# Forgetting attention and channel mix: x of the first two chunks written straight into SBUF, the first chunk mixed pair by pair

## Chip, cores, metric

One core of a Trainium2 chip. The metric is the device time of one execution in microseconds (us); lower is better. TensorE does the matrix products, VectorE (DVE), ScalarE (ACT) and GpSimd (POOL) the rest; SyncE (SP) issues nearly all DMAs. SBUF is the memory on the core, PSUM the banks that TensorE writes.

## What is computed

A causal attention with a forget bias, for 8 batches, 8 heads, 576 tokens and 64 columns a head; its output, laid out as 576 tokens of 512 columns, goes through a channel mix:

```python
s_pos = np.maximum(s, 0.0)
cum = np.cumsum(s_pos, axis=-1)
bias = -(cum[:, :, :, None] - cum[:, :, None, :])
scores = np.where(causal, -1000000000.0, scale * q @ k.T + np.minimum(bias, 0.0))
attn = softmax(scores)                       # over the keys
x = attn @ v                                 # then laid out as [batch, token, 512]
x_prev = x shifted by one token (zero first)
xk = mu_k * x + (1.0 - mu_k) * x_prev
xr = mu_r * x + (1.0 - mu_r) * x_prev
k = np.maximum(xk @ w_k, 0.0)                # 512 -> 1024
out = sigmoid(xr @ w_r) * (k * k @ w_v)      # 1024 -> 512
```

## The kernel before

**Attention.** It runs in visits; a visit is one batch and one pair of heads (`hp`, four pairs a batch). Batch 0 is visited in two halves: first the query tiles A (tokens 0 to 319) of all four pairs, then Z (tokens 320 to 575) of all four; the other batches are visited once a pair. A visit computes scores (`scores`, L815: products on TensorE at L828 or L839, then VectorE at L856, exponentials on ScalarE at L874, normalising on GpSimd at L893), turns the weights and multiplies by the values. For the first twelve visits the turning is done by TensorE (L982, L997) and the value products by L956; from visit 12 on by VectorE (L920) into the tile `turned` (`turned_d`, 128 x 3840 words), DMAs and L1133. `blanks` (L511) clears parts of `turned_d` once; in the kernel before it does so at the start.

**x.** `weighted` (L972) ends in a ScalarE copy (L1095) of the value products from the PSUM bank `po` into the SBUF tile `xT`: columns are tokens, the 128 partitions are the channels of the pair. `finish` (L1453) writes `xT` to `x_d` in DRAM by DMA (L1461).

**Channel mix.** The 4608 tokens are cut into 18 chunks of 256 (`CT`). A chunk can start when the attention of its tokens is there for all four pairs, for chunk 0 after the four A visits, for chunk 1 after the four Z visits. `channel_mix` (L1165) loads x of all pairs by DMA from `x_d` (L1355), mixes it (`mix`, L1233): for each block `c` of 128 channels (which is one pair of heads) ScalarE multiplies by mu into a PSUM bank (L1193), VectorE adds the shifted part (L1204); then `splits` takes two blocks at once, a ScalarE copy rounds them to the high part `xh` (L1223) and VectorE subtracts for the low part `xl` (L1227). `mix(0)` feeds the hidden layer (L1256, 96 products a chunk), `mix(1)` the gate (L1298). The hidden layer is squared (L1268 to L1286) into `kh` and `kl`, which have one buffer, and multiplied by w_v (L1328). The weights w_k, w_r and w_v arrive as float64 words and are converted once by ScalarE, VectorE and GpSimd (`load_weight`, L626: L661 to L695); those of w_v use the tiles `x` and `r` and the bank `xp` on the way.

**Order.** Nothing is emitted in program order: each step is a task with an engine, a length, what it reads and writes and a due time, and `Plan.run` (L322) lists the tasks forty times, forward and backward, by its own model of lengths and gaps, and emits the best order found. Each engine then runs its own queue in that order. While TensorE would have nothing to do, the planner puts in dummy products on the identity matrix (`plan.idle`, L445, into bank `xp`), until the task `plan.busy_from`, which is the first mix of chunk 0 (L1201). `late` (L1496) orders the loads of w_v behind the x load of chunk 0 in the plan.

Of the kernel before, what the change touches and what calls it, by code (L numbers as in the profile page):

```python
# [337 lines left out]
def forgetting_attention_then_channel_mix(  # L338
# [15 lines left out]
    nc = tc.nc  # L354
# [148 lines left out]
    turned_d = fixed(const.tile([P, 4, NS, 32], F32, name="turned"))  # L503
    across = fixed(ph_both[:, 0 : 4 * NS * 32].rearrange("p (i s x) -> p i s x", i=4, s=NS))
    across.last = phs

    def slots(h, kb, t):

# [20 lines left out]
                [], [(t, ("h", kb))], 64, 36,  # L529
            )  # L530

    first_load = []
    late, LATE = [], ("v",)
    mu = fixed(const.tile([P, 2, NC], F32, name="mu"))
    mu1 = fixed(const.tile([P, 2, NC], F32, name="mu1"))
# [433 lines left out]
        )  # L969
        plan.columns[i] = 4 * n  # L970

    def weighted(pts, V, xT, tiles, blocks):  # L972


        def transposed(pt, ph):
# [186 lines left out]

    x_d = [fixed(dram.tile([P, NP, S + 1], F32, name=f"x_d{b}")) for b in range(B)]

    def channel_mix(ch, start, span):  # L1165
        t0 = ch * CT
        segs = []
        t = t0
# [6 lines left out]
        last = ch >= NCHUNK - 3  # L1175

        def at(x):
            plan.due = start + span * x

        def product_bank():  # L1180
            if not last:
# [3 lines left out]

        def mixed(which, c, y, xm):
            for i, (_, _, n, o) in enumerate(segs):

                def to(n=n, o=o):
                    return xm.get()[:, y * CT + o : y * CT + o + n]  # L1190

                first = act(
                    lambda n=n, o=o, i=i, to=to: nc.scalar.activation(  # L1193
                        to(),
                        x.get()[:, c, o + i + 1 : o + i + 1 + n],
                        AF.Copy,
                        scale=mu.ap[:, which, c : c + 1],
                    ),
                    [(x, i), (mu, which)], [(xm, (y, o)), (xm, "a")], n, 160, ports="S>P",
                )  # L1200
                if plan.busy_from is None:  # L1201
                    plan.busy_from = first
                dve(
                    lambda n=n, o=o, i=i, to=to: nc.vector.scalar_tensor_tensor(  # L1204
                        out=to(),
                        in0=x.get()[:, c, o + i : o + i + n],
                        scalar=mu1.ap[:, which, c : c + 1],
                        in1=to(),
                        op0=ALU.mult,
                        op1=ALU.add,  # L1210
                    ),
                    [(x, i), mu1], [(xm, (y, o)), (xm, "d")], n, ports="SP>P",
                )

        def splits(c, xm, hi, lo):
            parts = [(xm, (y, o)) for y in range(2) for _, _, _, o in segs]
            cc = slice(c, c + 2)

            def src():
                return xm.get().rearrange("p (c x) -> p c x", c=2)  # L1220

            act(
                lambda: nc.scalar.copy(hi.get()[:, cc], src()),  # L1223
                parts, [(hi, c), (hi, c + 1)], 2 * CT, ports="P>S",
            )
            dve(
                lambda: nc.vector.tensor_tensor(  # L1227
                    out=lo.get()[:, cc], in0=src(), in1=f32(hi.get()[:, cc]), op=ALU.subtract
                ),
                parts + [(hi, c), (hi, c + 1)], [(lo, c), (lo, c + 1)], 2 * CT, ports="PS>S",  # L1230
            )
# [129 lines left out]
        if ch == 0:  # L1361
            first_load.append(i_x)
        at(-MLEAD)
        mix(0)
        for fp in range(NF // 2):
            at(0.1 * fp)
            hidden(fp)
            if fp == 0:
                at(0.2)
                mix(1)  # L1370
        for tt in range(CT // P):
            at(0.4 + 0.1 * tt)
            gate(tt)
# [64 lines left out]
    prefix_sums()  # L1438
    plan.due = 25000.0
    constant_rows()  # L1440
    plan.due = 50000.0
    blanks()
    plan.due = 1000.0
    load_mu()
    for o in range(DF // 512):
# [7 lines left out]
    def finish(pts, V, xT, n, due):  # L1453
        b, hp, tiles = visits[n]
        plan.due = due
        weighted(pts, V, xT, tiles, n >= BLOCKS)
        q0, q1 = QS[tiles[0]], QS[tiles[-1]] + QN[tiles[-1]]

        c = slice(1 + q0 if q0 else 0, 1 + q1)
        dma(  # L1460
            lambda: nc.sync.dma_start(x_d[b].ap[:, hp, c], xT.get()[:, c]),  # L1461
            [(xT, -1)] + [(xT, x) for x, _ in sums_of(tiles)],
            [(x_d[b], (hp, y)) for y in range(2) if tiles is ALL or y == (q0 > 0)],
            1300 * (q1 - q0) / S,
        )
        if hp == NP - 1:
            there[b] = q1

    for n, (b, hp, tiles) in enumerate(visits):
        due = dues[n]  # L1470
        step = STEPS[tiles]
        plan.due = due - LEAD * step
        if 0 < n < len(visits) - 1:
            load(n + 1)
        plan.due = due
        xT = sbuf([P, S + 1], "xT", 1)
        pool(lambda xT=xT: nc.gpsimd.memset(xT.get()[:, 0:1], 0.0), [], [(xT, -1)], 2, 36)
        for j in range(2):
            plan.due = due + j * step
            pt = scores(b, 2 * hp + j, tiles, n >= BLOCKS, *QKs[n])  # L1480
            if j == 0:
                other = pt
            else:
                finish((other, pt), Vs[n], xT, n, due + (j + WDUE) * step)
            if j == 0 and n + 1 < len(visits):
                plan.due = due + SPLIT * step
                prepare(n + 1)
        while done_chunks < NCHUNK:
            end = (done_chunks + 1) * CT - 1
# [4 lines left out]
            channel_mix(done_chunks, chunk_due, CHUNK)  # L1494
# [47 lines left out]
```

## Time and profile before

| what | value |
|---|---|
| runs | 794.86 us median of 3 (793.86 to 796.66) |
| profiled execution | 793.36 us, of which the span 791.5 us |
| TensorE busy | 771.6 us, 97% of the span |
| weight loads of TensorE | 638.7 us, 81% |
| VectorE, ScalarE, GpSimd busy | 563.8, 472.1, 345.1 us |
| mean granted TensorE clock | 0.994 of full |
| DMA | 152.12 MB, mean 192 GB/s |

The span runs from the first to the last instruction of the profiled execution. A busy time is the sum of the instructions' durations; products that follow one another overlap in it. The granted clock has two levels, full (2.4 GHz, shown as 1.00) and half (1.2 GHz, shown as 0.50); a figure between is a mean over a stretch. Lines are those of the kernel before.

### The profile page before, as it was taken

How to read it: one execution, taken by the hardware profiler on the slowest of the kernel's cores; microseconds unless marked ns; L12 is line 12 of the kernel's file. 1: busy time of each engine (PE TensorE's matmuls, PEld its weight loads, DVE VectorE, ACT ScalarE, POOL GpSimd, SP SyncE). 2: the span in 40 equal slices, each digit the busy share in tenths (PEclk: the TensorE clock that was granted, in tenths of full speed). 3: DMA queues.
4: the chain of work that ended last, by engine and by line, in shares of the span. 5: the costliest groups of instructions: out<-in, count | busy, mean ns of one | idle time of the engine just before them, and what ended most of it. 6: DMA issues, size and time to landing. Idle time of an engine off the chain costs nothing.

```text
span 791.5 us, 16205 instructions
## 1 busy us (share of the span) xinstructions
PE 771.6 (97%) x5216; PEld 638.7 (81%) x5216; DVE 563.8 (71%) x1868; ACT 472.1 (60%) x1305; POOL 345.1 (44%) x620
## 2 busy tenths in 40 slices
PE   7999989999999999999999999999999999999998
PEld 5667867978887878788878888887888788788997
DVE  7987976668866877677777677668877787355521
ACT  5778988766744665465564666556645666345411
POOL 7996887543544444423344434343444421100000
PEclk9998999999999999999999999999999999999999
DMA  7887875688999888888888988899888776421000
GB/s 226 261 251 217 246 215 149 179 194 219 227 233 243 230 209 226 210 223 212 224 203 210 233 218 220 212 246 217 238 228 213 185 196 172 115 76 41 14 27 27
DMA packets 65701, 152.12 MB, mean 192 GB/s; under 512 B 13662, under 2 KB 27236, under 8 KB 65616
## 3 DMA queue, kind: packets, MB, share of 16 engines
q1 hardware_dynamic: 65456, 150.92, 73.4%
q8 instruction: 41, 0.67, 0.4%
q14 instruction: 44, 0.36, 0.1%
q10 hardware_dynamic: 160, 0.16, 0.1%
HBM read 51.34 MB, written 19.48 MB: 89 GB/s over the span
## 4 chain that ended last, share of the span: by engine, by line
PE 56%; SPq 12%; DVE 11%; DMA 6%; POOL 6%; ACT 5%; issue 4%; DVEq 0%; ACTq 0%; POOLq 0%
PE m L1256 16%; PE m L1328 12%; SPq L1104 11%; PE s L839 6%; PE po L1133 5%; PE m L1298 5%; DVE turned L920 3%; DMA ph<-turned 2%; POOL W L893 2%; DVE W L856 2%; PE po L956 2%; DVE xp L1204 2%; PE s L1328 2%; DMA x<-x_d 2%; ACT xp L1193 2%
## 5 line engine op out<-in xcount | busy, mean ns | idle before, releaser
L874 ACT ACTIVATE W<-W,nm 128x448 f32<-128x448 f32 (+4 forms) x320 | 178.6, 559 | 75.4 <-DVE nm L856 71.6
L1256 PE MATMUL m<-xh,w_k 128*128 128x256 f32 x1024 | 198.8, 283 | 0.5 <-DVE g L1338 0.5
L893 POOL TENSOR_SCALAR W<-W,rinv 128x192 f32<-128x192 f32 (+4 forms) x320 | 164.5, 529 | 26.8 <-DVE rinv L942 25.2
L1328 PE MATMUL m<-w_v,kh 128*128 128x512 f32 (+1 forms) x512 | 171.4, 394 | 0.0
L1256 PEld LDWEIGHTS m<-xh,w_k 128*128 128x128 f32 x1024 | 163.0, 188 | 2.9 <-DVE g L1338 0.9
L856 DVE CUSTOM_DVE_ANT_0 W<-s,causal 128x448 f32<-128x448 f32 (+5 forms) x320 | 130.4, 419 | 45.9 <-PE s L839 40.1
L1256 PE MATMUL m<-xl,w_k 128*128 128x256 f32 x512 | 144.1, 282 | 0.0
L920 DVE STREAM_TRANSPOSE turned<-W 128x64 f32<-128x64 f32 (+5 forms) x432 | 121.8, 327 | 28.8 <-DMA ph<-turned 11.7
L1193 ACT ACTIVATE xp<-x,mu 128x256 f32<-128x256 f32 (+3 forms) x172 | 72.4, 421 | 59.8 <-DMA x<-x_d 26.3
L1328 PEld LDWEIGHTS m<-w_v,kh 128*128 128x128 f32 x512 | 94.9, 189 | 15.4
L937 POOL TENSOR_SCALAR rinv<-sums 128x5 f32<-128x5 f32 (+2 forms) x72 | 17.2, 238 | 199.6 <-ACT W L874 193.2
L839 PE MATMUL s<-KH,G 128*64 128x64 f32 x336 | 98.1, 303 | 5.3 <-DVE nm L856 4.2
L1328 PE MATMUL m<-w_v,kl 128*128 128x512 f32 (+1 forms) x256 | 101.3, 396 | 0.0
L839 PE MATMUL s<-KL,G 67*64 67x64 f32 x336 | 98.4, 296 | 0.0
L1256 PEld LDWEIGHTS m<-xl,w_k 128*128 128x128 f32 x512 | 96.5, 189 | 1.0
L1204 DVE SCALAR_TENSOR_TENSOR xp<-x,mu,xp 128x256 f32<-128x256 f32 (+3 forms) x172 | 70.8, 411 | 32.4 <-ACT xp L1193 30.2
L1298 PE MATMUL m<-w_r,xh 128*128 128x512 f32 x256 | 87.4, 399 | 0.0
L839 PEld LDWEIGHTS s<-KH,G 128*64 128x64 f32 x336 | 60.2, 180 | 20.6 <-DVE nm L856 15.0
L796 POOL TENSOR_TENSOR G<-raw,KH 128x1152 fp32r<-128x1152 f32 x28 | 75.0, 2679 | 2.0
L1133 PE MATMUL po<-ph,V 128*64 128x64 f32 (+4 forms) x768 | 67.1, 327 | 1.0 <-DMA KL<-cum_d 0.9
L839 PEld LDWEIGHTS s<-KL,G 67*64 67x64 f32 x336 | 60.2, 180 | 7.0
L1133 PEld LDWEIGHTS po<-ph,V 128*64 128x64 f32 x768 | 39.6, 137 | 26.8 <-issue 21.6
(137 smaller groups left out, 1244.0 us busy)
## 6 DMA issues: line engine op xcount, KB each, us to landing
ph<-turned SPq DMA_DIRECT2D x384, 120.0 KB
raw<-in_q SPq DMA_DIRECT2D x28, 576.0 KB
G<-KH SPq DMA_DIRECT2D x56, 288.0 KB
V<-in_v SPq DMA_DIRECT2D x32, 320.0 KB
out<-g SPq DMA_DIRECT2D x35, 256.0 KB
x_d<-xT SPq DMA_DIRECT2D x28, 288.5 KB
KL<-G SPq DMA_DIRECT2D x28, 288.0 KB
KH<-KH SPq DMA_DIRECT2D x28, 288.0 KB
```

The costliest lines, as they stand in the source:

```text
L839: lambda x=x, g=g, K=K: nc.tensor.matmul(ps.get()[:m, :w], g.get()[: 64 + PIECES if x else P, h % 2, q0 : q0 + m], K.get()[: 64 + PIECES i ...
L856: lambda a=a, e=e, at=at, i=i: nc.vector.tensor_tensor_reduce(out=W.ap[:m, at : at + e - a], in0=ps.get()[:m, a - k0 : e - k0], in1=causal ...
L874: lambda: nc.scalar.activation(W.ap[:m, :n], W.ap[:m, :n], AF.Exp, bias=nm.get()[:m, 3 * t + mi : 3 * t + mi + 1], scale=-1.0, accum_out=s ...
L893: lambda: nc.gpsimd.tensor_scalar(out=to(), in0=W.ap[:m, :n], scalar1=rinv.get()[:m, t : t + 1], scalar2=1.0, op0=ALU.mult, op1=ALU.mult,),
L920: lambda a=a, e=e, g=g, n=n: nc.vector.transpose(at(a, e, g), W.ap[:m, P * a : P * a + n].rearrange("p (k g x) -> p k g x", g=g, x=32),),
L1104: lambda g=g, i=i: nc.sync.dma_start(across.get()[32 * g : 32 * g + 32, i], turned_d.get()[32 * i : 32 * i + 32, g]),
L1133: nc.tensor.matmul(to, V.get()[:, kb, j], x, start=ps is rest or kb == 0, stop=ps is rest or kb == NQ - 1 or t == NQ - 1, skip_group_check ...
L1193: lambda n=n, o=o, i=i, to=to: nc.scalar.activation(to(), x.get()[:, c, o + i + 1 : o + i + 1 + n], AF.Copy, scale=mu.ap[:, which, c : c + 1],
L1204: lambda n=n, o=o, i=i, to=to: nc.vector.scalar_tensor_tensor(out=to(), in0=x.get()[:, c, o + i : o + i + n], scalar=mu1.ap[:, which, c : ...
L1256: lambda u=u, f=f, c=c, n=n, w=w, x=x: nc.tensor.matmul(ps.get()[:, u * CT : (u + 1) * CT], weight["k", c, f // 4].get()[:, w, f % 4 * P : ...
L1298: lambda c=c, n=n, x=x, w=w: nc.tensor.matmul(ps.get(), x.get()[:, c, ts], weight["r", c, 0].get()[:, w], start=c == 0 and n == 0, stop=c ...
L1328: lambda f=f, n=n, x=x, w=w, ps=ps, ms=ms: nc.tensor.matmul(ps.get()[:, :m], x.get()[:, f, ts], weight["v", f, 0].get()[:, w, ms], start=f ...
```

## The change

x of chunks 0 and 1 no longer goes through DRAM. Two tiles `placed`, each 4 blocks of 258 columns, are laid into the storage of `turned_d`, which has no other use until visit 12; `blanks` moves to that visit and waits for the last reader of them. For batch 0 the ScalarE copies of `weighted` write into them: an A visit copies 256 columns for chunk 0 and 65 for chunk 1 instead of 320 to `xT`, a Z visit 192 for chunk 1 and 65 to `xT`, of which only those 65 are written to DRAM, for chunk 2. The writes of the A visits and the x loads of chunks 0 and 1 are gone. Chunk 0's `mix(0)` becomes a generator: after each A visit the block of that pair is mixed and split by itself (256 columns at a time instead of 512), in the bank `po`; the rest of chunk 0 follows as before. `plan.busy_from` becomes the first mix of `mix(1)` of chunk 0, and the loads of w_v are ordered behind that task.

```diff
+    IN_PLACE = 2
+    placed = [
+        fixed(
+            turned_d.ap.rearrange("p g s x -> p (g s x)")[:, i * NC * (CT + 2) : (i + 1) * NC * (CT + 2)]
+            .rearrange("p (c x) -> p c x", c=NC)
+        )
+        for i in range(IN_PLACE)
+    ]
+    turned_d.last = placed
...
         for (a, e), ps in zip(spans, (rest, po)[-len(spans) :]):
-            act(
-                lambda a=a, e=e, ps=ps: nc.scalar.copy(xT.get()[:, 1 + a : 1 + e], ps.get()[:, 0 : e - a]),
-                [ps], [(xT, a)], e - a, ports="P>S",
-            )
+            for x, part, c, a0, a1 in [(xT, a, 0, a, e)] if hp is None else direct(xT, hp, a, e):
+
+                def to(x=x, c=c, a0=a0, a1=a1):
+                    return x.get()[:, c + a0 + 1 : c + a1 + 1] if x is xT else x.get()[:, hp, c + a0 + 1 : c + a1 + 1]
+
+                act(
+                    lambda ps=ps, to=to, a=a, a0=a0, a1=a1: nc.scalar.copy(to(), ps.get()[:, a0 - a : a1 - a]),
+                    [ps], [(x, part)], a1 - a0, ports="P>S",
+                )
+
+    def direct(xT, hp, a, e):
+
+        for ch, x in enumerate(placed):
+            a0, a1 = max(a, ch * CT - 1), min(e, (ch + 1) * CT)
+            if a0 < a1:
+                yield x, hp, -ch * CT, a0, a1
+        if e == S:
+            yield xT, a, 0, IN_PLACE * CT - 1, S
...
-                if plan.busy_from is None:
+                if plan.busy_from is None and which:
                     plan.busy_from = first
...
             st[which] = (hi, lo)
+            if ch == 0 and which == 0:
+                for c in range(NC):
+                    xm = bank(1, "po", 1)
+                    mixed(which, c, 0, xm)
+                    splits(c, xm, hi, lo, 1)
+                    yield
+                return
             for c in range(0, NC, 2):
...
-        at(-XLEAD)
-        x = sbuf([P, NC, CT + 2], "x")
-        for i, (b, a, n, o) in enumerate(segs):
-            i_x = dma(
+        if ch < IN_PLACE:
+            x = placed[ch]
+            if ch == 0:
+                yield from mix(0)
+        else:
+            at(-XLEAD)
+            x = sbuf([P, NC, CT + 2], "x")
+        for i, (b, a, n, o) in enumerate(segs if ch >= IN_PLACE else ()):
+            dma(
...
-        if ch == 0:
-            first_load.append(i_x)
-        at(-MLEAD)
-        mix(0)
+        if ch:
+            at(-MLEAD)
+            yield from mix(0)
...
+        if b == 0:
+            ch = int(q0 > 0)
+            if ch == 0:
+                pool(lambda: nc.gpsimd.memset(placed[0].get()[:, hp, 0:1], 0.0), [], [(placed[0], hp)], 2, 36)
+            if ch == 0:
+                if hp == 0:
+                    chunks[ch] = channel_mix(ch)
+                next(chunks[ch])
+                return
...
+        if n == BLOCKS:
+            plan.due = due
+            blanks()
...
     for i in late:
-        plan.behind[i] = {first_load[0]}
+        plan.behind[i] = {plan.busy_from}
```

## Rows read from the trace of the kernel before

**Rows 1.** Page, busy us (share of the span) and instructions of TensorE and others.

```profile
PE 771.6 (97%) x5216; PEld 638.7 (81%) x5216; DVE 563.8 (71%) x1868; ACT 472.1 (60%) x1305; POOL 345.1 (44%) x620
```

**Rows 2.** Busy us (instructions) by stage, then granted clock, DMA share, GB/s.

```profile
43.70:65.86 22.16, 21.36 (x121) 12.67 (x120) 18.13 (x59) 17.33 (x50) 20.18 (x29) 0.85 0.79 239
200.00:690.00 490.00, 483.70 (x3336) 405.02 (x3336) 362.67 (x1241) 284.49 (x763) 202.73 (x363) 1.00 0.86 215
...
20.00:45.00 25.00, 23.23 (x156) 15.17 (x153) 23.01 (x81) 19.63 (x76) 23.87 (x48) 1.00 0.85 248
45.00:57.00 12.00, 11.47 (x74) 7.09 (x72) 11.53 (x39) 8.91 (x28) 11.44 (x18) 1.00 0.84 252
57.00:73.00 16.00, 15.24 (x83) 10.08 (x83) 11.19 (x34) 13.85 (x37) 9.27 (x14) 0.79 0.82 250
73.00:87.00 14.00, 14.00 (x123) 13.05 (x122) 13.52 (x43) 10.58 (x32) 10.59 (x15) 1.00 0.88 249
```

**Rows 3.** The same view (PE, PEld, DVE, ACT, POOL) in slices of 2 us.

```profile
62.00:64.00 2.00, 2.00 (x11) 1.16 (x12) 1.21 (x3) 2.00 (x6) 2.00 (x2) 0.50 0.55 122
...
102.00:104.00 2.00, 1.00 (x6) 0.62 (x5) 1.68 (x7) 1.96 (x10) 1.65 (x6) 0.95 0.79 184
104.00:106.00 2.00, 1.97 (x7) 0.84 (x9) 1.63 (x6) 2.00 (x9) 2.00 (x4) 0.50 0.85 265
```

**Rows 4.** Chain of work that ended last: start us, us, what.

```profile
58.57 3.58 PE s L828 x6
62.15 3.61 PE po L956 x20
...
78.23 1.89 PE po L956 x20
```

**Rows 5.** Timeline of TensorE: start us, us, engine, line, operation, tiles, count.

```profile
42.51 1.20 PE L956 MATMUL po<-ph,V 128*64 128x320 f32 x12
...
49.78 1.40 PE L828 MATMUL s<-KH,G 65*128 65x288 f32 x4
...
55.23 0.49 PE L445 MATMUL xp<-ident 128*128 128x256 bf16 x3
...
65.86 0.53 PE L1256 MATMUL m<-xh,w_k 128*128 128x256 f32 x1
```

**Rows 6.** Timeline of ScalarE around chunk 0's first mix.

```profile
46.35 0.43 ACT L1095 COPY xT<-po 128x320 f32<-128x320 f32 x1
...
57.76 0.46 ACT L1193 ACTIVATE xp<-x,mu 128x256 f32<-128x256 f32 x1
...
62.43 0.67 ACT L874 ACTIVATE W<-W,nm 128x448 f32<-128x448 f32 x1
```

**Rows 7.** Timeline of SyncE's DMA queue: start us, us to issue, what.

```profile
41.98 0.43 SPq L618 DMA_DIRECT2D mu<-in_moe_mu_k  x1
...
47.95 0.33 SPq L1461 DMA_DIRECT2D x_d<-xT  x1
...
51.04 0.63 SPq L1355 DMA_DIRECT2D x<-x_d  x1
```

**Rows 8.** GpSimd: the clears of `blanks` (ns min/median/max), and a wait from its timeline.

```profile
L516 POOL MEMSET turned<- x2: 368/368/369, 7.9 to 8.2; 128x320 f32 x2
...
72.65 0.23 POOL L937 TENSOR_SCALAR rinv<-sums 128x2 f32<-128x2 f32 x1 [5.29 <-ACT W L874]
```

**Rows 9.** ScalarE copies by form, 10 to 130 us: busy us, mean ns, idle before.

```profile
L1023 ACT COPY ph<-t 128x256 f32<-128x256 f32 x21 | 7.8, 369 | 2.0 <-PE t L982 1.8
L1052 ACT COPY ph<-t 64x64 f32<-64x64 f32 x32 | 6.6, 207 | 0.9 <-PE t L982 0.6
```

**Rows 10.** VectorE: a subtraction's form; a mix and a transpose from its timeline.

```profile
L1227 DVE TENSOR_TENSOR xl<-xp,xh 128x512 fp32r<-128x512 f32 x2 | 1.4, 688 | 0.4 <-ACT xh L1223 0.4
...
132.01 0.48 DVE L1204 SCALAR_TENSOR_TENSOR xp<-x,mu,xp 128x256 f32<-128x256 f32 x1
...
152.28 1.24 DVE L920 STREAM_TRANSPOSE turned<-W 128x128 f32<-128x128 f32 x4
```

More of the change, by code (lines that the diff above doesn't have):

```diff
@@ L530, in zero @@
             )
-    first_load = []
     late, LATE = [], ("v",)
@@ L970, in both_heads, with weighted @@
         plan.columns[i] = 4 * n
-    def weighted(pts, V, xT, tiles, blocks):
+    def weighted(pts, V, xT, tiles, blocks, hp):
         def transposed(pt, ph):
@@ L1163, in forgetting_attention_then_channel_mix, with channel_mix @@
     x_d = [fixed(dram.tile([P, NP, S + 1], F32, name=f"x_d{b}")) for b in range(B)]
-    def channel_mix(ch, start, span):
+    def channel_mix(ch):
         t0 = ch * CT
@@ L1177, in at @@
         def at(x):
-            plan.due = start + span * x
+            plan.due = times[ch] + CHUNK * x
         def product_bank():
@@ L1187, in mixed @@
             for i, (_, _, n, o) in enumerate(segs):
+                source = (x, c) if ch < IN_PLACE else (x, i)
                 def to(n=n, o=o):
@@ L1211, in mixed, with splits @@
                     ),
-                    [(x, i), mu1], [(xm, (y, o)), (xm, "d")], n, ports="SP>P",
+                    [source, mu1], [(xm, (y, o)), (xm, "d")], n, ports="SP>P",
                 )
-        def splits(c, xm, hi, lo):
-            parts = [(xm, (y, o)) for y in range(2) for _, _, _, o in segs]
-            cc = slice(c, c + 2)
+        def splits(c, xm, hi, lo, k=2):
+            parts = [(xm, (y, o)) for y in range(k) for _, _, _, o in segs]
+            cc = slice(c, c + k)
             def src():
[L1220 to L1225, printed above, removed]
+                return xm.get()[:, : k * CT].rearrange("p (c x) -> p c x", c=k)
+            his, los = [[(z, c + y) for y in range(k)] for z in (hi, lo)]
+            act(lambda: nc.scalar.copy(hi.get()[:, cc], src()), parts, his, k * CT, ports="P>S")
             dve(
@@ L1369, in channel_mix @@
                 at(0.2)
-                mix(1)
+                yield from mix(1)
         for tt in range(CT // P):
@@ L1440, in forgetting_attention_then_channel_mix @@
     constant_rows()
-    plan.due = 50000.0
-    blanks()
     plan.due = 1000.0
@@ L1455, in finish @@
         plan.due = due
-        weighted(pts, V, xT, tiles, n >= BLOCKS)
+        weighted(pts, V, xT, tiles, n >= BLOCKS, hp if b == 0 else None)
         q0, q1 = QS[tiles[0]], QS[tiles[-1]] + QN[tiles[-1]]
-        c = slice(1 + q0 if q0 else 0, 1 + q1)
+        if hp == NP - 1:
+            there[b] = q1
+        if b == 0:
[7 more added lines that the diff above has]
+                return
+        c = slice(1 + IN_PLACE * CT - 1 if b == 0 else 0, 1 + q1)
         dma(
             lambda: nc.sync.dma_start(x_d[b].ap[:, hp, c], xT.get()[:, c]),
-            [(xT, -1)] + [(xT, x) for x, _ in sums_of(tiles)],
+            [(xT, -1)] * (b > 0) + [(xT, x) for x, _ in sums_of(tiles)],
             [(x_d[b], (hp, y)) for y in range(2) if tiles is ALL or y == (q0 > 0)],
@@ L1465, in finish @@
         )
-        if hp == NP - 1:
-            there[b] = q1
+    chunks, times = {}, {}
     for n, (b, hp, tiles) in enumerate(visits):
@@ L1475, in forgetting_attention_then_channel_mix @@
         plan.due = due
-        xT = sbuf([P, S + 1], "xT", 1)
-        pool(lambda xT=xT: nc.gpsimd.memset(xT.get()[:, 0:1], 0.0), [], [(xT, -1)], 2, 36)
+        xT = sbuf([P, S + 1], "xT", 1) if b or tiles == Z else None
+        if b:
+            pool(lambda xT=xT: nc.gpsimd.memset(xT.get()[:, 0:1], 0.0), [], [(xT, -1)], 2, 36)
         for j in range(2):
@@ L1493, in forgetting_attention_then_channel_mix @@
             chunk_due = max(chunk_due + CHUNK, due + 2 * step + (MARGIN if end >= S else EARLY_MARGIN))
-            channel_mix(done_chunks, chunk_due, CHUNK)
+            times[done_chunks] = chunk_due
+            for _ in chunks.pop(done_chunks, None) or channel_mix(done_chunks):
+                pass
             done_chunks += 1
     for i in late:
-        plan.behind[i] = {first_load[0]}
+        plan.behind[i] = {plan.busy_from}
     with tc.manual_schedule():
```

4 lines of the change are left out of this document (2 added, 2 removed).

## Prediction

> **What bounds the kernel now.** I read the busy shares first, then the busy times by stage, then the chain of work that ended last, and last the timelines of the single engines around the first chunk.
>
> TensorE is busy for 97% of the span [rows 1], and from 200 to 690 us it is busy 483.70 of 490 us at the full clock [rows 2]. So after the start the chunk products and the attention products share a TensorE that has hardly a gap: what is saved has to be saved as lost TensorE time, and that lies early. Busy time alone hides it. From 43.70 to 65.86 us TensorE counts 21.36 of 22.16 us as busy, but the mean clock is 0.85 there [rows 2]; dummy products run until 55.7 us [rows 5], and from 60 to 66 us the granted clock is 0.50, the lower of its two levels (1.2 GHz; a slice of it stands in [rows 3]).
>
> The reader is to see a second thing in the stages: GpSimd is busy 11.44 of 12 us from 45 to 57, but only 9.27 of 16 and 10.59 of 14 us in the next two stages, and VectorE falls from 11.53 of 12 to 11.19 of 16 in the first of them [rows 2]. Those two engines prepare the weights and the attention weights. Their idle time from 57 to 87 us (GpSimd 6.73 + 3.41 = 10.1 us) is the slack that a better order of chunk 0 could win back; it can't win back more than that there, because none of GpSimd's work in it is removed.
>
> The chain passes through this stage as a score group of 3.58 us and a value group of 3.61 us; a later value group takes 1.89 us [rows 4]. The DMA of x is not a piece of this chain here. The way of chunk 0's x is long all the same: last copy from PSUM at 46.35 us [rows 6], write to DRAM issued at 47.95, load issued at 51.04 [rows 7], first mix at 57.76 [rows 6], first hidden product at 65.86 [rows 5].
>
> **The change part by part.**
>
> *The round trip through DRAM.* For chunk 0 the write and the load go. From the end of the last copy (46.35 + 0.43 = 46.78) to the first mix there are 11.0 us. Chunk 0 can be mixed, but for its last pair, before that copy; so hidden products can begin near 50 us and not at 65.86. As this path isn't on the chain, I count nothing for its length itself; what counts is what the earlier start changes on the chain, in the next two terms. What is late next is GpSimd: the casts of the weights and the normalised tiles.
>
> *The half clock.* The dummies end where the first mix is planned. The change moves that mark to the first mix for the gate, and it puts real products (96 of the hidden layer) where TensorE now has little to do. The groups of 3.58 and 3.61 us ran at the lower level. At the upper one a group of four of the same line takes 1.40 us [rows 5], so I set six at 2.10 (their widths may differ), and the value group takes 1.89 [rows 4]. 7.19 - 2.10 - 1.89 = 3.20 us on the chain. The Trainium skill says in "TensorE: Matmul & The Clock Gate" (Part 1: The HAM clock gate) that the lowered clock is the default state and that activity releases it. The trace agrees as far as it goes, since the clock fell behind the last dummies; by that rule the 3.20 us come back, and if the fall had another cause the sum would be 1.8 us and not 5.0.
>
> *The burst of mixing.* After the x load ScalarE runs four mixes for the hidden layer (0.46 us the first of them) and two casts among the attention's instructions, and the exponentials of a tile whose scores were ready earlier start at 62.43 us [rows 6]. GpSimd then waits 5.29 us for exponentials until 72.65 us [rows 8]. A cast of 512 columns is some 0.58 us by the two copies of rows 9 (0.84 ns a column on top of 0.15 us: an estimate), so the burst is 4 x 0.46 + 2 x 0.58 = 3.0 us of ScalarE. Three pairs of four leave it, so I count 2.3 us. Bounds: 0, if the gate's mix fills the same place; 10.1 us less the 3.2 above, 6.9, if all of GpSimd's idle time from 57 to 87 goes. I take 2.3 since it is the row of this very burst.
>
> *More and smaller instructions.* ScalarE: a copy of 320 columns (0.43 us [rows 6]) becomes one of 256 and one of 65 (0.369 + some 0.207 [rows 9]), 0.15 us more, four times; the copies of the later half split likewise, four times; four casts of 256 columns for two of 512 cost 4 x 0.369 - 2 x 0.58 = 0.3. Together 1.5 us on an engine that is busy 8.91 of 12 us in the tighter stage [rows 2]: no cost while its work beside is there, 1.5 if not. VectorE: four subtractions of 256 for two of 512. The whole one takes 0.688 us; the half has no row. Bounds are half of that, 0.34, and 0.48, the mix of 256 columns [rows 10]; that row is the nearest, as its shape is the half's: 4 x 0.48 - 2 x 0.69 = 0.5 us more. Also 3 x (0.48 + 0.48) = 2.9 us of VectorE for the first three pairs move into the stage from 20 to 45 us, which has 2.0 us free of 25 [rows 2]. 0.9 + 0.5 = 1.4 us may be pushed on, but GpSimd is the tighter one there (23.87 of 25). I take 0.5, bounds 0 and 1.5.
>
> *The product bank.* The mix of pairs holds the bank of the value products (po) until its cast and subtraction are done, so the next pair's value products queue behind it on TensorE, and the dummies and transposes behind those. Today the bank of the last pair of the first half waits from its products at 42.51 us [rows 5] to its copy at 46.35 [rows 6] with nothing behind it in a hurry; a mix adds two instructions of some 0.48 us and two of 0.4 to 0.5, say 2 us. Cost 0 if the planner draws copy and mix ahead of weight work, since 3.8 us of waiting can be cut by the 2; else up to 2 us a pair.
>
> *mu.* Its two loads are issued at 41.98 us and after [rows 7]; now the first pair needs them near 21 us. On SyncE's queue they pass the loads of weights, keys and queries between, 0.43 us each; the queue isn't full, cost 0, bound 0.9 us.
>
> *blanks.* Four clears of the transposed tile (two of them 0.368 us [rows 8]) move from the start to after chunk 1's last mix, since x of chunks 0 and 1 lies in that tile. Chunk 1's last mix ran at 132.01 us and the tile is first written at 152.28 [rows 10]. GpSimd's stretch between covers them: 0. They would cost if chunk 1 were mixed later than some 150 us.
>
> *Chunk 1 in place.* Its x is there earlier, but its hidden products have to wait for chunk 0's output products, which have the only buffer of the squared hidden layer and wait for w_v. I count 0; it could give more (below). w_v is now ordered behind the gate's first mix and not behind the x load at 51.04 us: about the same time, 0.
>
> Sum: 3.2 + 2.3 - 0.5 = 5.0 us. The profiled execution took 793.36 us (span 791.5 and 1.86 around it), which gives 788.4; it is 1.5 us under the median of the runs, 794.86, so the forecast is 789.9 us.
>
> **The rivals.**
> 1. *The hole only moves.* Hidden products run early and TensorE lacks them later; w_v and the attention, GpSimd's and VectorE's work, come no sooner. For it: both engines are nearly full from 20 to 57. Against it: 10.1 us idle on GpSimd after that. Gain 0 to 1: 794.4 us.
> 2. *The half clock comes later, and longer* (slower). With hidden and gate products used up early, from 75 to 110 us only attention is left until w_v is ready, and the dummies are over. The clock already fell there once: TensorE was busy 1.00 of 2 us from 102 to 104, and 0.50 was granted from 104 to 106 [rows 3]. It decides if the busy share from 80 to 100 us sinks to that of 102 to 104. Three dips of the price above, 9.6, less the 3.2 of the old one: 6.4 us more, 801.3 us. Against it: the planner keeps late work as filler.
> 3. *All of GpSimd's slack is won*: 10.1 us, 784.8 us. For it: chunk 1's x in place could also fill the hole at 102 us [rows 3].
> 4. *The change does less than it says*: the planner lists the first three pairs' mixes as late as the last pair, and the burst stays. Only the clock's 3.2 us come back: 791.7 us.
>
> **How the numbers follow.** Forecast 0.44, rival 1 0.16, rival 2 0.14, rival 3 0.17, rival 4 0.09. The planner makes a new order for the whole kernel, in which 490 us with 6.3 us of gaps can win or lose a few us; that widens each case by some 3 us. A measurement of this kernel can tell about 0.3% (2.4 us) from no change. Forecast and rivals 3 and 4 give most of faster, 0.60; rival 1 and the near edges of the forecast and of rival 4 give same, 0.22; rival 2 and the bad edge of rival 1 give slower, 0.18. The range reaches from rival 3's time less some 2 us, 783, to 798, past rival 1 with its spread; what is left out is rival 2 (0.14) and a low tail of some 0.05.
>
> **What would show it.** First hidden product near 50 us; no slice at 0.50 from 58 to 66; GpSimd's idle time from 57 to 87 us cut by about 5; output products of chunk 0, and the end of the last value group, earlier by about 5. A hidden layer that starts early with output products at the old time is rival 1; a clock of 0.50 over more than 10 us from 70 to 110 is rival 2. The prediction is wrong if first mixes come at 46 us and later, if value products wait for po, or if the stretch from 200 to 690 us changes by more than the start does.

## The result, and the profile after

The changed kernel took 808.42 us (median of 4 runs, 802.45 to 811.19) against 794.36 us for the kernel before on the same chip (793.22 to 796.66): a ratio of 1.0142 with a 95% interval of 1.0095 to 1.0188. It is slower: the whole interval lies above 1. The forecast was 789.9 us, with 798 as the upper end of the range; sign and range are both wrong. A ratio is not the quotient of the two medians; the two differ by up to some 0.4% (here the quotient is 1.0177). The ratios leave out slow executions, those over 1.5% above the fastest of their kernel, which are two of the kernel before with a gap of 1005 and two of the changed kernel with WAIT 152, the profiled one among them (both kernels below).

The profiled execution took 807.62 us, its span 805.8. The page of the changed kernel, first the busy times, then the granted clock in 40 slices of 20 us:

```profile
PE 781.5 (97%) x5157; PEld 650.5 (81%) x5157; DVE 565.7 (70%) x1870; ACT 471.3 (58%) x1315; POOL 344.2 (43%) x616
...
PEclk9768999999999999999999999999999999999999
```

TensorE has 59 instructions fewer than in [rows 1] and is busy 9.9 us longer. The 59 are dummies (61 for 120), so the same work has got slower. The clock fell in the second, third and fourth slices, 20 to 80 us. The stages show more. They count busy us (instructions) of PE, PEld, DVE, ACT and POOL, then granted clock, DMA share and GB/s. The kernel before:

```profile
28.00:70.00 42.00, 40.04 (x249) 25.77 (x246) 35.43 (x115) 32.90 (x105) 36.61 (x60) 0.92 0.84 252
...
85.00:125.00 40.00, 37.49 (x248) 28.77 (x246) 32.41 (x117) 34.14 (x107) 34.17 (x54) 0.96 0.69 197
```

and the changed kernel, with its GpSimd stage from 57 to 87 us and the long stage answering to [rows 2]:

```profile
28.00:70.00 42.00, 38.80 (x171) 24.57 (x172) 36.47 (x120) 31.59 (x113) 34.43 (x60) 0.67 0.75 250
57.00:87.00 30.00, 29.42 (x191) 22.87 (x190) 25.33 (x73) 21.06 (x61) 20.35 (x28) 0.85 0.76 243
85.00:125.00 40.00, 36.71 (x241) 29.46 (x240) 33.95 (x112) 32.46 (x97) 33.55 (x44) 0.96 0.50 129
...
200.00:690.00 490.00, 478.26 (x3284) 403.13 (x3284) 364.90 (x1253) 285.64 (x773) 205.25 (x368) 0.99 0.85 213
```

From 28 to 70 us the mean clock is 0.67 and not 0.92: 42 x 0.33 = 13.9 us of full-speed TensorE time are missing in place of 3.4. In the long stage TensorE is idle 11.7 us of 490, in [rows 2] it was 6.3. The first difference, 10.5 us, is no delay as it stands, since a matmul at half speed costs nothing where TensorE would have waited or run dummies. The delay can be counted in real products, that is without the dummies; there are 5096 of them in every kernel here. TensorE alone up to 200 us (busy us, instructions, granted clock, DMA share, GB/s), in the kernel before and in the changed one:

```profile
0.00:200.00 200.00, 189.51 (x1275) 0.97 0.78 215
...
0.00:200.00 200.00, 191.00 (x1174) 0.92 0.69 198
```

That makes 1275 - 120 = 1155 and 1174 - 61 = 1113 real products, 42 fewer. From 200 to 690 us it is 3284 for 3336, 52 fewer. At the 6.8 a us of the long stage before (3336 in 490 us) these are some 6 and 8 us, an estimate that adds up to the 14.3 us between the spans. So more than half of the loss against this execution of the kernel before arises after 200 us, at a clock of 0.99.

Part of the early loss is older than the fall of the clock: the first value group of the changed kernel starts at 25.33 us, the dummies still running, and in the kernel before here:

```profile
19.72 1.20 PE L956 MATMUL po<-ph,V 128*64 128x320 f32 x12
```

Why the clock fell is in the timelines. TensorE in the changed kernel (start us, us, engine, line, operation, tiles, count):

```profile
25.33 1.20 PE L964 MATMUL po<-ph,V 128*64 128x320 f32 x12
...
28.46 0.29 PE L445 MATMUL xp<-ident 128*128 128x256 bf16 x1
...
35.52 2.19 PE L964 MATMUL po<-ph,V 128*64 128x320 f32 x12
...
67.17 0.50 PE L1284 MATMUL m<-xh,w_k 128*128 128x256 f32 x1
```

and ScalarE:

```profile
27.85 0.47 ACT L1216 ACTIVATE po<-turned,mu 128x256 f32<-128x256 f32 x1
...
28.78 0.48 ACT L1216 ACTIVATE xp<-turned,mu 128x256 f32<-128x256 f32 x1
...
43.72 0.47 ACT L1216 ACTIVATE xp<-turned,mu 128x256 f32<-128x256 f32 x1
```

The mix at 27.85 is the first pair's, for the hidden layer. The one at 28.78, in bank xp, is the first mix for the gate, which ends the dummies. It needs only x of its own block, that is of the first pair, and that pair has just come; the planner listed it at once. The gate itself is far off, and the mix then holds xp half filled until the second pair's x at 43.72. So the last dummy runs at 28.46 us instead of 55.23 [rows 5] (61 dummies in all for 120), before three of the four value groups. The next value group of the same shape takes 2.19 us for 1.20. The clock in slices of 5 us:

```profile
35.00:40.00 5.00, 5.00 (x20) 2.78 (x19) 3.79 (x13) 3.25 (x14) 4.47 (x12) 0.50 0.45 171
40.00:45.00 5.00, 5.00 (x19) 2.87 (x19) 4.51 (x14) 3.65 (x13) 3.69 (x6) 0.50 0.80 254
...
55.00:60.00 5.00, 4.42 (x15) 2.51 (x14) 4.47 (x14) 4.51 (x16) 2.93 (x6) 0.50 0.88 265
```

Hidden products begin at 67.17 us, no earlier than the 65.86 of [rows 5].

### The profile page after: what moved, and what is told of

Its sections match the earlier page's. It is cut to its first block, busy times and chain, and to the rows that moved or that the text cites. A ratio compares the mean times of both kernels' runs of the same rounds, so it can differ in the third digit from the quotient of the medians.

```text
span 805.8 us, 16055 instructions
## 1 busy us (share of the span) xinstructions
PE 781.5 (97%) x5157; PEld 650.5 (81%) x5157; DVE 565.7 (70%) x1870; ACT 471.3 (58%) x1315; POOL 344.2 (43%) x616
## 4 chain that ended last, share of the span: by engine, by line
PE 67%; DVE 10%; SPq 7%; DMA 7%; issue 3%; ACT 3%; POOL 2%; DVEq 0%; POOLq 0%; ACTq 0%
PE m L1284 16%; PE m L1356 15%; PE s L847 8%; PE m L1326 7%; SPq L1126 7%; PE po L1155 5%; PE s L836 4%; DMA x<-x_d 3%; DVE turned L928 3%; PE po L964 3%; DMA ph<-turned 3%; PE s L1356 2%; DVE W L864 2%; DVE xp L1227 2%; PE s L1284 1%
## 5 line engine op out<-in xcount | busy, mean ns | idle before, releaser
L882 ACT ACTIVATE W<-W,nm 64x64 f32<-64x64 f32 (+4 forms) x320 | 178.4, 559 | 73.7 <-DVE nm L864 69.5
L1284 PE MATMUL m<-xh,w_k 128*128 128x256 f32 x1024 | 202.1, 286 | 0.2 <-DVE kl L1313 0.2
L864 DVE CUSTOM_DVE_ANT_0 W<-s,causal 64x64 f32<-64x64 f32 (+5 forms) x320 | 130.6, 419 | 63.0 <-PE s L847 50.4
L1356 PE MATMUL m<-w_v,kh 128*128 128x512 f32 (+1 forms) x512 | 173.2, 400 | 0.0
L1284 PEld LDWEIGHTS m<-xh,w_k 128*128 128x128 f32 x1024 | 165.0, 191 | 3.3 <-DVE kl L1313 0.7
L928 DVE STREAM_TRANSPOSE turned<-W 128x64 f32<-128x64 f32 (+5 forms) x432 | 121.8, 328 | 26.4 <-DMA ph<-turned 10.3
L847 PE MATMUL s<-KH,G 128*64 128x64 f32 x336 | 98.1, 305 | 11.6 <-DVE nm L864 11.4
L1216 ACT ACTIVATE xp<-x,mu 128x256 f32<-128x256 f32 (+3 forms) x160 | 66.7, 417 | 64.4 <-DMA x<-x_d 34.6
L1227 DVE SCALAR_TENSOR_TENSOR xp<-x,mu,xp 128x256 f32<-128x256 f32 (+3 forms) x160 | 64.8, 405 | 33.1 <-ACT xp L1216 30.8
```

The source lines that it names most:

```text
L847: lambda x=x, g=g, K=K: nc.tensor.matmul(ps.get()[:m, :w], g.get()[: 64 + PIECES if x else P, h % 2, q0 : q0 + m], K.get()[: 64 + PIECES i ...
L864: lambda a=a, e=e, at=at, i=i: nc.vector.tensor_tensor_reduce(out=W.ap[:m, at : at + e - a], in0=ps.get()[:m, a - k0 : e - k0], in1=causal ...
L882: lambda: nc.scalar.activation(W.ap[:m, :n], W.ap[:m, :n], AF.Exp, bias=nm.get()[:m, 3 * t + mi : 3 * t + mi + 1], scale=-1.0, accum_out=s ...
L928: lambda a=a, e=e, g=g, n=n: nc.vector.transpose(at(a, e, g), W.ap[:m, P * a : P * a + n].rearrange("p (k g x) -> p k g x", g=g, x=32),),
L1216: lambda n=n, o=o, i=i, to=to: nc.scalar.activation(to(), x.get()[:, c, o + i + 1 : o + i + 1 + n], AF.Copy, scale=mu.ap[:, which, c : c + 1],
L1284: lambda u=u, f=f, c=c, n=n, w=w, x=x: nc.tensor.matmul(ps.get()[:, u * CT : (u + 1) * CT], weight["k", c, f // 4].get()[:, w, f % 4 * P : ...
```

## The experiments

Each kernel ran beside the kernel before on the same chip; a ratio is to that one. A kernel named "before" below differs from the kernel before, all others from the changed kernel. The planner's constants HEAD (spacing of visits), WAIT (price of a stall) and the gap after a DMA change the order alone, not the work.

**The changed kernel again.**

> The changed kernel once more, unchanged, as the control of the next three on the same chip. All theories: 802 to 811 us as before. Open in it is the start: in the first profile the dummy products took 0.42 us each (the lower clock) from 2 to 23 us, where the kernel before ran them at 0.27 us from about 5 us on. If that is chance of one execution, this profile shows short ones again; if it belongs to this order of work, it shows 0.42 us again.

807.01 us, ratio 1.0125 (1.0062 to 1.0188). Its clock from 28 to 70 us is 0.56, the last dummy runs at 24.44 us. The loss stands in a second study. The open question about the start is answered: the same eleven dummies took 2.56 us in the first profile and 1.37 us in this one, so the slow start was that of one execution and not of the order.

```profile
22.16 2.56 PE L445 MATMUL xp<-ident 128*128 128x256 bf16 x11
...
18.26 1.37 PE L445 MATMUL xp<-ident 128*128 128x256 bf16 x11
```

The first value group starts at 21.57 us here. By 200 us this execution has 25 real products fewer than the kernel before (1191 - 61 = 1130), from 200 to 690 us 67 fewer (3269): some 4 and 10 us.

**The gate's first mix held back.** In `splits` the cast of the fourth pair is kept, and the first mix for the gate is ordered behind it, so the dummies can run on:

```diff
+            i = act(lambda: nc.scalar.copy(hi.get()[:, cc], src()), parts, his, k * CT, ports="P>S")
+            if k == 1:
+                hold[0] = i
...
+    plan.behind[plan.busy_from] = {hold[0]}
```

> The changed kernel, with one more rule for the planner: the first mix for the gate, which ends the dummy products, is listed only behind the cast of the last pair's block. Theory 1 (dummies end too early: the gate's first block needs only the first pair's x, its mix runs at 28.8 us, and TensorE falls to half clock from 33 to 46 and 53 to 66 us): dummies go on to about 48 us, no stretch at 0.50 before 60 us, first hidden product near 50 us, 788 to 796 us. Theory 2 (the pairs' mixes in the bank of the value products and on full engines delay the attention): value products of the first four visits still at 25, 35, 43, 52 us, 800 us or more. Theory 3 (the new order is worse in many places): about 800, with no stretch that carries it.

801.54 us, ratio 1.0038 (0.9997 to 1.0079). My theory 1 had the cover right and the time, 788 to 796 us, wrong. The last dummy is at 55.63 us (121 dummies), and the stages are:

```profile
28.00:70.00 42.00, 39.88 (x270) 26.98 (x269) 38.84 (x127) 36.05 (x125) 38.00 (x62) 1.00 0.87 256
...
57.00:87.00 30.00, 29.91 (x220) 24.43 (x220) 28.20 (x77) 22.88 (x62) 24.35 (x30) 1.00 0.83 249
85.00:125.00 40.00, 37.99 (x247) 29.83 (x246) 33.65 (x122) 35.99 (x112) 33.80 (x55) 0.91 0.58 149
...
200.00:690.00 490.00, 482.00 (x3322) 404.74 (x3321) 364.74 (x1246) 286.40 (x768) 205.90 (x367) 1.00 0.86 215
```

The half clock from 28 to 70 is gone altogether, and hidden products begin at 61.66 us. Real products are 9 behind the kernel before at 200 us (1267 - 121 = 1146), and 14 more from 200 to 690 us (3322):

```profile
0.00:200.00 200.00, 189.27 (x1267) 0.98 0.74 202
```

GpSimd's idle time from 57 to 87 is 30 - 24.35 = 5.7 us against 10.1 in [rows 2], shorter by 4.5. That is the early gain I had forecast, and still the kernel isn't faster than before. The output products begin at 102.78 us (before: 110.63), but the first attention visit of the later kind (turned by VectorE and DMA) begins its value products at 185 us, against 186 before: nothing of it is left. Where it is given back shows between 95 and 100 us:

```profile
95.00:100.00 5.00, 4.00 (x16) 2.64 (x18) 5.00 (x17) 4.22 (x15) 3.34 (x8) 0.56 0.29 64
```

VectorE is busy all 5 us there; six of its instructions are the conversion of w_v, which the output products need, such as

```profile
96.14 1.28 DVE L681 TENSOR_SCALAR m<-m 128x512 int32<-128x512 int32 x2
...
97.88 0.68 DVE L685 SCALAR_TENSOR_TENSOR m<-w_v,m 128x512 int32<-128x512 int32 x1
```

On TensorE the gate's products are used up at 91.85 us and the output products begin at 102.78; between them lies no product of the channel mix, and a value group runs at half speed (its equal at 85.40 us took 1.96). Just before, TensorE waits 0.75 and 1.18 us for VectorE's maxima of the scores (L864):

```profile
91.85 0.39 PE L1328 MATMUL m<-w_r,xh 128*128 128x512 f32 x1
...
96.00 0.74 PE L847 MATMUL s<-KH,G 128*128 128x448 f32 x1 [1.18 <-DVE nm L864]
...
97.52 3.68 PE L964 MATMUL po<-ph,V 128*64 128x256 f32 x20
...
102.78 0.46 PE L1358 MATMUL m<-w_v,kh 128*128 128x512 f32 x1
```

**The kernel before with short dummies.** Nothing of the change but its early end of the dummies: `busy_from` is the second visit's copy to `xT` (73 dummies, the last at 28.13 us).

```diff
+            copies.append(act(
...
+            if len(copies) == 2:
+                plan.busy_from = copies[1]
```

> The kernel before with one edit: the dummy products end at the second visit's copy of x (29 us) and not at chunk 0's first mix (57.8 us). x still goes through DRAM and nothing is mixed by pairs. Theory 1: this alone costs most of the loss, half clock from about 33 us on, 800 to 808 us. Theories 2 and 3: the dummies matter little, 793 to 798 us.

811.78 us, ratio 1.0174 (1.0125 to 1.0222), somewhat over the 800 to 808 us of theory 1. In this order the early end alone costs as much as the whole change, or more; by 200 us 111 real products are missing (1117 - 73 = 1044), some 16 us:

```profile
28.00:70.00 42.00, 36.62 (x154) 21.15 (x152) 32.17 (x106) 28.03 (x92) 31.56 (x54) 0.70 0.68 211
```

**In place, but not by pairs.** Chunk 0's x stays in SBUF, but its mix for the hidden layer runs in two blocks after all four pairs, and that mix ends the dummies again:

```diff
-                if plan.busy_from is None and which:
+                if plan.busy_from is None:
...
-                    xm = bank(1, "po", 1)
-                    mixed(which, c, 0, xm)
-                    splits(c, xm, hi, lo, 1)
                     yield
-                return
+                at(-MLEAD)
```

> The changed kernel without the mixing by pairs: x of chunks 0 and 1 still in place, chunk 0's hidden mix in blocks of two after all four pairs as in the kernel before, dummies until that mix. Theory 1: dummies until about 47 us, full clock till there, 785 to 794 us (the round trip gone, nothing lost). Theory 2: the same. Theory 3: near 800.

804.54 us, ratio 1.0057 (1.0023 to 1.0091): 99 dummies, the last at 48.95 us, and a clock that lies between, as high as that of the kernel before:

```profile
28.00:70.00 42.00, 38.35 (x227) 24.48 (x226) 37.35 (x124) 34.76 (x115) 38.32 (x64) 0.92 0.81 239
```

In these four kernels the two whose dummies end before 29 us are the slowest; two orders further down do not follow this. Writing x in place brings no gain here either, where theories 1 and 2 had 785 to 794 us.

**Other orders of the same work.** Each edit above also makes the planner draw another order of the whole kernel, so I asked what an order is worth alone. The kernel before with HEAD 11150 for 11200, and with a gap after a DMA of 1005 for 1000:

> The kernel before with one planner constant moved by less than half a per cent (HEAD 11200 to 11150 ns, a due time); the work is the same, but the planner emits another order. Theory 3 (a new order by itself costs time, whatever the change was): 0.5 to 1.5% slower than before, 798 to 812 us. Theory 4 (what is left over before in the changed kernel with the gate's mix held back comes from the change itself): within 0.3% of before.

> The kernel before with another planner constant moved (the gap after a DMA, 1000 to 1005 ns); 106 dummy products instead of 120, another order from the 38th TensorE instruction on. Theory 3: 0.5 to 1.5% slower than before. Theory 4: within 0.3%, or a little more for the fewer dummies.

793.24 us, ratio 0.9885 (0.983 to 0.994), and 804.13 us, ratio 1.0012 (0.9968 to 1.0055). A constant changed by 0.4% moved the kernel before by more than the whole gain I had forecast (5.0 us, 0.6%), if these four executions are taken at their word (they are repeated below). It moved it down, which neither theory had; the second constant stayed within 0.3%. Then the held kernel with HEAD 11150, and with WAIT 152 for 150:

> The changed kernel with the gate's first mix held behind the last pair (as in e1_hold), and HEAD 11150 ns: another order of the same work, 128 dummies for 121. Theory 3: this draws a time of its own between 0.5% under and 1.5% over before, and the mean of the three held kernels is that of the kernels before with a moved constant. Theory 4: all held kernels lie near +0.4%.

> The same held kernel with the planner's constant WAIT at 152 instead of 150: a third order of the same work, 134 dummies. Theory 3: a time of its own, 0.5% under to 1.5% over before. Theory 4: near +0.4%.

797.1 us, ratio 0.9958 (0.9923 to 0.9993), and 803.85 us, ratio 1.0055 (1.0019 to 1.0092). So not all held kernels lie near +0.4%, as theory 4 had it; each order has a time of its own. The clock from 28 to 70 us is 1.00 in both. In the first, hidden products begin where the prediction had them, near 50 us:

```profile
51.15 0.35 PE L1286 MATMUL m<-xh,w_k 128*128 128x256 f32 x1
```

In both the clock from 85 to 125 us is 0.91, as in the first held kernel: the hole there isn't an accident of one order. But neither does it come from the change: the kernel before has 0.96 there under its own constants, and 0.91 with HEAD 11150 (0.96 in its second profile), with the gap of 1005 and with WAIT 152 (below), in this order:

```profile
85.00:125.00 40.00, 38.66 (x246) 30.16 (x245) 31.73 (x112) 31.14 (x97) 36.41 (x54) 0.91 0.69 175
...
85.00:125.00 40.00, 36.05 (x224) 28.68 (x223) 31.84 (x110) 30.32 (x96) 32.58 (x49) 0.91 0.86 230
...
85.00:125.00 40.00, 37.99 (x256) 29.79 (x255) 33.10 (x114) 32.87 (x101) 32.02 (x51) 0.91 0.77 212
```

Last the partners that were missing, the changed kernel not held under both constants, and the kernel before with WAIT 152:

> The changed kernel with HEAD 11150, which only draws another order of the same work. It is the partner of the held kernel with HEAD 11150 (ratio 0.9958 to the kernel before) and of the kernel before with HEAD 11150 (0.9885). Theory that the early end of the dummies costs about 0.9% whatever the order: last dummy near 28 us, a clock of 0.50 in several 5 us slices from 30 to 66, ratio 0.9958 + 0.009 = 1.005 (1.001 to 1.009). Rival, that what the hold won was itself a lucky order: no dearer than the held one, 0.990 to 0.999.

> The changed kernel with WAIT 152, again only another order; partner of the held kernel with WAIT 152 (1.0055). Theory that the early end of the dummies costs about 0.9%: last dummy near 28 us, half clock between 30 and 66, ratio 1.0145 (1.010 to 1.019). Rival, luck of the order: 1.000 to 1.008.

> The kernel before with WAIT 152: the third order of the kernel before, so that each order constant has the kernel before, the changed one and the held one. Theory that the change without the early end of the dummies is worth nothing that shows above the luck of the order: the held kernel (1.0055) is within 0.8% of this one, so 0.998 to 1.013. Rival, that writing in place and mixing by pairs costs time of itself even with the dummies held: this one is 0.99 or less, as the order with HEAD 11150 (0.9885) was against its held partner (0.9958).

799.63 us, ratio 1.0008 (0.9972 to 1.0044); 802.7 us, ratio 1.0019 (0.998 to 1.0058); 798.25 us, ratio 0.9996 (0.9958 to 1.0034). The last dummies of the first two are at 31.41 and 31.23 us, so the early end is a property of the change in every order tried. My 0.9% for it is not: with HEAD 11150 holding wins 0.50%, and the two intervals still touch; with WAIT 152 the held kernel is no faster than the other. What holding wins in all three orders is an early lead, in one profile each: by 200 us there are 1146 real products for 1113 and 1130, 1161 for 1144, and 1133 for 1103, some 2 to 5 us. That is not far above the scatter: two executions of one program, the kernel before with HEAD 11150, differ by 16 products there (1140 and 1156). The kernel before with WAIT 152 is near 1, as my theory for it had it. In the first of the two changed kernels the clock fell less, for a reason that I did not follow up:

```profile
28.00:70.00 42.00, 39.30 (x225) 25.27 (x223) 37.51 (x123) 34.47 (x117) 35.44 (x59) 0.88 0.79 238
```

**The best one once more.**

> The kernel before with HEAD 11150 once more, on another chip and in more executions, since it is the only one that beat both kernels, by 1.15% in four executions. If the gain belongs to the order that it drew: 0.983 to 0.994 again, mean clock near 0.99. If it was luck of the executions (the runs of the kernel before scatter from 794 to 806): 0.996 to 1.002.

797.02 us, ratio 0.9961 (0.9926 to 0.9995). It beats the kernel before again, by 0.4% and not by 1.15%: the first four executions were lucky ones. It is the kernel before with another order and has nothing of the change.

**All runs together.** Much of the difference goes with the clock. Over the 88 executions of the kernel before in the four studies of these experiments (794.16 to 806.35 us, mean granted clock 0.976 to 0.994) time and clock go together with a correlation of -0.79, 6.1 us for each 0.01 of clock. The median is 799.4 us at 0.989. A kernel's ratio times 800 us gives its difference; 6.1 us for each 0.01 below 0.989 is the part that goes with the clock; the rest is what else the order and the work are worth. The first row is the least sure, since its study is not among the four: the kernel before took 794.36 us there, and the clocks of those executions, but for the profiled one with 0.994, aren't on record.

| kernel | ratio | median clock | difference, us | with the clock | rest |
|---|---|---|---|---|---|
| changed, first result | 1.0142 | 0.970 | +11.4 | +11.5 | -0.2 |
| changed, again | 1.0125 | 0.972 | +10.0 | +10.3 | -0.3 |
| changed, HEAD 11150 | 1.0008 | 0.983 | +0.6 | +3.6 | -3.0 |
| changed, WAIT 152 | 1.0019 | 0.980 | +1.5 | +5.8 | -4.2 |
| held | 1.0038 | 0.988 | +3.0 | +0.6 | +2.4 |
| held, HEAD 11150 | 0.9958 | 0.990 | -3.4 | -0.3 | -3.1 |
| held, WAIT 152 | 1.0055 | 0.985 | +4.4 | +2.4 | +2.0 |
| before, HEAD 11150 | 0.9885, 0.9961 | 0.992, 0.989 | -9.2, -3.1 | -1.5, 0 | -7.7, -3.1 |
| before, WAIT 152 | 0.9996 | 0.988 | -0.3 | +0.6 | -0.9 |
| before, gap 1005 | 1.0012 | 0.984 | +1.0 | +3.3 | -2.4 |
| before, short dummies | 1.0174 | 0.970 | +13.9 | +11.5 | +2.4 |
| in place, not by pairs | 1.0057 | 0.982 | +4.6 | +4.2 | +0.3 |

The part with the clock is 3.6 to 11.5 us where the dummies end near 28 to 31 us and -0.3 to 2.4 us where they are held; it is 3.3 and 4.2 us in two kernels whose dummies end at 62 and 49 us. The rest lies between -8 and +2.4 us in all families alike. It is a regression and not an experiment: what makes TensorE wait also lowers its clock, so the two columns are not quite independent. The two edits that move the dummies and leave the work as it is (held, and the kernel before with short dummies) bear the first column out, as far as one order each can; nothing bears out a gain of the change in the last.

## Why the prediction was wrong

- **The half clock: the step that failed.** I wrote that the change "moves that mark to the first mix for the gate, and it puts real products (96 of the hidden layer) where TensorE now has little to do", and booked 3.2 us of gain. I had taken the gate's mix to come about when hidden products do: for the loads of w_v I put it at "about the same time" as 51.04 us. The diff says otherwise: for chunk 0 a mix reads `(x, c)`, one pair's x, so the first one for the gate can be listed as soon as the first pair is in, and was, at 28.78 us. The mark moved 27 us forward and not to the end of the pairs. In place of 3.2 us won, the clock from 28 to 70 us sank from 0.92 to 0.67, and by 200 us the changed kernel is 42 and 25 real products behind in its two profiles (some 6 and 4 us), with the gate's mix held 9 (some 1 us). The kernel before with only this edit loses 1.74%. The source of the mark had to be looked up as the source of a transfer is; I costed the dummies as cover without asking what ends them. The Trainium skill, which I named there ("TensorE: Matmul & The Clock Gate", Part 1: The HAM clock gate), calls the lowered clock the default that activity releases; the traces agree, with 0.67, 0.56 and 0.70 in the three profiles above whose dummies ended before 29 us and 1.00 in those of the three held kernels. It was applied to the wrong moment. Nor do late dummies assure the clock: the kernel before with WAIT 152 had them until 62 us and 0.84 from 28 to 70 us.
- **The long stage.** The larger part of the 14 us, 52 and 67 real products or some 8 and 10 us, was lost from 200 to 690 us at a clock of 0.99 and 1.00. My own sign of being wrong ("if the stretch from 200 to 690 us changes by more than the start does") came true. No run shows the cause; see the new order, below.
- **The round trip.** Hidden products "can begin near 50 us": they began at 67.17 in the changed kernel, but at 61.66, 51.15 and 49.84 in the held ones. The first of the three shows little, since the kernel before with HEAD 11150 begins them at 61.95 and 58.78 us in its two profiles. The dependence was read rightly; it came to bear in two orders, both held.
- **The burst.** I forecast GpSimd's idle time from 57 to 87 us shorter by about 5. In the changed kernel it is 30 - 20.35 = 9.7 us, nearly unchanged; in the held kernel it is shorter by 4.5. The other two held kernels, with 6.9 and 8.9 us, are shorter by 3.3 and 1.2, and the changed kernel with HEAD 11150, whose dummies end early, has 3.7, shorter by 6.4. So the size was met in some orders and not in others, whatever the dummies do, and in the held kernel it was worth nothing at the end: see the next point.
- **The rivals.** Rival 2 (the half clock comes later) named the mechanism of what stays once the dummies are held: hidden and gate products used up early, w_v not ready, 0.91 from 85 to 125 us in three orders. I had given it 9.6 us and let it decide; it is 40 x 0.09 = 3.6 us of full-speed time, against 1.6 before, and the kernel before has the same 3.6 in profiles of three other orders. Rival 1 (the hole only moves) describes the held kernels best: outputs begin 8 to 17 us earlier than before, and the ratios are 1.0038, 0.9958 and 1.0055; part of the lead belongs to the order, since the kernel before with HEAD 11150 begins them at 104.79 and 101.17 us. What is late next, in the first held kernel, is VectorE with the maxima and the conversion of w_v. None of my rivals was the half clock at the old place, longer; that case was missing.
- **More and smaller instructions, po, blanks.** These held. The copies of 256 and 65 columns took 373 and 217 ns for 369 and 207, the half cast 364 for 369, and the half subtraction 410, in the middle of my bounds of 340 and 480:

```profile
L1248 DVE TENSOR_TENSOR xl<-po,xh 128x256 fp32r<-128x256 f32 x4 | 1.6, 410 | 0.4 <-ACT xh L1246 0.4
...
L1246 ACT CAST xh<-po 128x256 fp32r<-128x256 f32 x4 | 1.5, 364 | 0.0
L1108 ACT COPY turned<-po 128x256 f32<-128x256 f32 x4 | 1.5, 373 | 4.5 <-PE po L964 4.5
...
L1108 ACT COPY turned<-po 128x65 f32<-128x65 f32 x4 | 0.9, 217 | 0.0
```

  (columns: busy us, mean ns, idle before it and its releaser). No wait for po stands among TensorE's waits from 28 to 70 us. The clears run at 130.56 us behind chunk 1's last mix, and `turned` is first written at 163.1.
- **The new order.** I allowed 3 us for it. With one constant of the planner moved the same work took 0.9885, with another 1.0012, some 10 us apart (4 by the repeated run, 0.9961). In the changed kernel's long stage TensorE waits for the maxima of the scores twice as long as before (3.5 us, 6 times, there):

```profile
PE s L847 <- DVE nm L864: 8.4, 8, 2.6
```

  (us in total, times, longest). Is that the change or the draw? The stage has 478.26 busy us here, 475.33 in the second profile of the same kernel, 480.98 and 479.49 under the two other constants, and 482.0 in all three held ones, but 477.12 in the kernel before with the gap of 1005, which does only 3279 products there. Even two executions of one program differ there: 3350 and 3315 products for the kernel before with HEAD 11150, some 5 us. So the draw, and in part the execution, can do it without the change; whether they did is open.
- **What stays open.** Whether writing in place and mixing by pairs costs or gains something of itself. Against the kernel before under the same constant the held kernels are 0.4, 0.7 (0 with the repeated run of its partner) and 0.6% slower; with the same constant the orders aren't the same, so this hints at a small cost and shows none. Dummies that run on into the hole at 95 us were not tried, since bank xp is in use by then. The cause of the loss after 200 us is open too.

## What to carry to other kernels

Where something fills TensorE's gaps to hold its clock, find the instruction that ends the filling and what that instruction waits for; a change that makes its inputs early ends the cover early, however little time the change itself takes. Tie such a mark to the work that is to take over (here the hidden products), not to a step that only used to stand beside it. To say where time went, count finished work by stage, without fillers; a clock or a busy share is no delay by itself. With a planner that re-orders everything, draw a few orders of either version by a harmless constant before believing a difference under 1%.

## What the runs showed of the hardware

The clock at the start differs between executions of one program. The first 19 dummies, in the same place in every kernel, took 3.53 and 4.24 us in the two profiled executions of the kernel before with HEAD 11150, 3.69 us in the profile of before and 4.24 in that of after:

```profile
1.82 4.24 PE L445 MATMUL xp<-ident 128*128 128x256 bf16 x19 [1.82 <-POOL ident masks.py:199]
```

In the profile of after, seven later dummies took 1.70 us together at 9.90 us, twice the pace of before (seven in 0.93 us at 6.90), although the granted clock of that stretch is shown as 1.00: up to its first recorded change that column can't be relied on, the durations can. The same program also differs later. In its two profiled executions the kernel before with HEAD 11150 had this from 28 to 70 us, first in the one that took less time in all (794.09 and 796.92 us), so the clock of this stretch alone doesn't decide the time:

```profile
28.00:70.00 42.00, 40.50 (x234) 26.99 (x232) 36.14 (x112) 29.71 (x94) 31.21 (x54) 0.84 0.79 244
```

```profile
28.00:70.00 42.00, 38.15 (x259) 25.93 (x256) 38.34 (x116) 33.08 (x101) 34.51 (x56) 1.00 0.79 245
```

The kernel before had a median of 794.36 us in the study of the result and of 799.4 us in the four later ones. So the profile that the prediction rests on, 793.36 us at a clock of 0.994, was one of its quicker executions.
